# Moving a tenth of the exponentials of a two-attention kernel from ScalarE to VectorE

## The chip, the cores and the metric

One core of one Trainium2 chip. The metric is device time in microseconds (us). The kernel before takes 1167.58 us (median of four runs, 1166.66 to 1175.48). Each experiment ran in the same rounds as the kernel before, on one chip, and its ratio compares the fast runs of these rounds. The batches of experiments ran on four chips, on which the median of the kernel before was 1166.6 to 1171.4 us; times set beside each other across batches carry that difference. With one core, "slow" means only that a run lies over 1.5% above the fastest of its kernel.

## The reference

Two attention blocks over 2048 positions with a model width of 512 and 32 heads of 16. Block A is full attention; block B is causal with a window of 256. Cut to what matters:

```python
qkv = (x @ wqkv).reshape(B, S, 3, H, Dh).transpose(2, 0, 3, 1, 4)
q, k, v = qkv[0], qkv[1], qkv[2]
scores = jnp.einsum("bhqd,bhkd->bhqk", q, k) * (Dh ** -0.5)
# block B only: scores = jnp.where(mask, scores, -1e9), mask: 0 <= i - j < 256
p = softmax(scores, axis=-1)
o = jnp.einsum("bhqk,bhkd->bhqd", p, v)
out = o.transpose(0, 2, 1, 3).reshape(B, S, D) @ wo
# the outputs of A and B are joined along the last axis
```

A head is only 16 wide, so that the 32 x 2048 x 2048 exponentials of block A, not the matmuls, are the large number.

## The kernel before

Work is cut into jobs: one head, one tile of 128 keys, 512 queries. Three jobs make a *slot*: three banks of scores, one exponential over 128x1536, three weight tiles. Two slots of scores lie in PSUM (six banks), one bank holds the output accumulator `op`, and one bank, `ms`, serves everything else: projections, guards, output projections. That work is doled out in *steps* between the slots.

```python
def scores(self, slot):
    sps = self.ps.tile([P, SLOT, 512], FP32, name="sps", tag="sps", bufs=2)
    for b, jb in enumerate(slot["jobs"]):
        r = slice(32 * jb.j, 32 * jb.j + KR)          # one of four 32-row groups
        ...
        if b == 0 and self.filled < 2:                # warm-up: whole array, overwritten
            self.nc.tensor.matmul(sps[:, 0, 0:WARM], lhsT=kT[:, gg, k0:k0 + P],
                                  rhs=qT[:, gg, 0:WARM], start=True, stop=True)
        for kt, q0, q1, o in jb.subs:
            self.nc.tensor.matmul(sps[:, b, o:o + q1 - q0], lhsT=kT[r, gg, k0:k0 + P],
                                  rhs=qT[r, gg, q0:q1], start=True, stop=True,
                                  tile_position=(32 * jb.j, 0))

def exps(self, slot):
    ...
    nc.scalar.activation(out=pT[:, b:e, :n], in_=sps[:, b:e, :n], func=ACT.Exp, scale=SCALE)
    ...                                               # block B: masks, on VectorE and GpSimd

def run(self):
    ...
    for s, sl in enumerate(slots):
        self.exps(sl)
        if s + 2 < len(slots):
            self.scores(slots[s + 2])
        self.values(...)                              # weights x values, into op
        ...                                           # what is due; then steps through bank ms:
        while credit >= 1.0 and self.fill(s, tasks, done):
            credit -= 1.0
            self.filled += 1
```

A projection step is two matmuls over the whole 128x128 array; two steps fill the bank, and VectorE evacuates it. VectorE and TensorE take their instructions in the order in which the kernel issues them, as the timeline below shows: the evacuation of `op`, whose last values had ended at 383.55 us, starts at 385.90 us, after two passes issued ahead of it, and the next values start at 386.63 us, after the evacuation has ended at 386.58 us.

## Time and profile before

| | before |
|---|---|
| time | 1167.58 us |
| ScalarE busy | 1098.6 us, 94% |
| ScalarE idle before its exponentials | 32.8 us |
| VectorE busy | 298.2 us, 25% |
| mean granted TensorE clock | 0.939 |

Two more parts turned out to matter. First, from the page of the kernel before, the busy tenths of TensorE in 40 slices of the span, and the granted TensorE clock in tenths of full speed:

```profile
PE   6788888878878887777778787787777887788893
...
PEclk9999899998999898999999999999999999976777
```

TensorE is busy 79% of the time, so it has a fifth in reserve, and its clock is near full nearly everywhere (0.939 on average). Second, the largest TensorE groups of the kernel before (out<-in, shapes, count | busy us, mean ns of one | idle before, and what ended it):

```profile
L457 PE MATMUL sps<-qTa,kTa 128*128 128x512 bf16 x659 | 261.0, 396 | 159.2 <-ACT pT L480 152.9
L462 PE MATMUL sps<-qTa,kTa 32*128 32x512 bf16 x2048 | 286.5, 404 | 1.5 <-ACT pT L480 1.5
```

The first are the warm-up matmuls, whose result is thrown away; they take nearly as long as all score matmuls of block A together, because three score matmuls mostly run beside each other in different 32-row groups of the array (2048 of them at 404 ns are 827 us, in 286.5 us of busy time; three or more overlap in the records for 264 us of it). TensorE's idle time ends with ScalarE: it waits for ScalarE, not the other way.

### The profile page before, as it was taken

What the parts mean: (1) busy time and instruction counts of PE and PEld (TensorE: products, weight loads), DVE (VectorE), ACT (ScalarE), POOL (GpSimd) and SP (SyncE); (2) the same over time, 40 slices, a digit from 0 to 9 for tenths busy, and PEclk for the clock granted to TensorE, in tenths of its full rate; (3) what the DMA queues carried; (4) which work ended last, traced back from release to release, by engine and by line L of the source; (5) the groups of instructions that cost most, each with busy time, mean ns of one, the idle gap of its engine ahead of it and who ended that gap; (6) DMA issues with size and microseconds to landing.
All of it is one profiled execution on the core that took longest, in us unless ns stands there. A gap on an engine that the chain in (4) does not pass through costs nothing.

```text
span 1169.9 us, 17451 instructions
## 1 busy us (share of the span) xinstructions
PE 926.1 (79%) x6844; PEld 270.6 (23%) x6944; DVE 298.2 (25%) x674; ACT 1098.6 (94%) x841; POOL 119.0 (10%) x316
## 2 busy tenths in 40 slices
PE   6788888878878887777778787787777887788893
PEld 3222222222222222222222222222222222222221
DVE  3442121132123222222322232224223132320101
ACT  3789999998999999999999999999999999999992
POOL 4000000010001001011200121102112011210100
PEclk9999899998999898999999999999999999976777
DMA  6022421221222112211220221124012112210101
GB/s 207 10 77 75 99 83 41 61 63 52 65 78 76 45 42 65 70 47 61 83 66 32 75 76 54 39 68 118 26 48 65 65 65 69 66 43 18 57 19 55
DMA packets 72810, 73.87 MB, mean 63 GB/s; under 512 B 22688, under 2 KB 55832, under 8 KB 72728
## 3 DMA queue, kind: packets, MB, share of 16 engines
q1 hardware_dynamic: 69656, 68.83, 19.3%
q10 hardware_dynamic: 2432, 1.84, 0.5%
q0 software_dynamic: 640, 2.10, 0.5%
q8 instruction: 54, 0.88, 0.3%
q14 instruction: 28, 0.23, 0.1%
HBM read 39.06 MB, written 31.58 MB: 60 GB/s over the span
## 4 chain that ended last, share of the span: by engine, by line
ACT 62%; PE 21%; issue 11%; DVE 3%; DMA 1%; POOL 0%; ACTq 0%; another core or an unknown queue 0%; SPq 0%; DVEq 0%; POOLq 0%
ACT pT L480 61%; PE sps L462 6%; PE sps L457 6%; PE ms L202 4%; PE op L514 4%; DVE va L285 1%; DVE osb L533 1%; PE ms L591 0%; DMA den<-od 0%; DVE pT L491 0%; DMA rb<-rd 0%; PE sps L358 0%; ACT xT L610 0%; DVE padmax L394 0%; DVE kTa L392 0%
## 5 line engine op out<-in xcount | busy, mean ns | idle before, releaser
L480 ACT ACTIVATE pT<-sps 128x1536 bf16<-128x1536 f32 (+4 forms) x827 | 1088.4, 1566 | 32.8 <-PE sps L462 31.1
L457 PE MATMUL sps<-qTa,kTa 128*128 128x512 bf16 x659 | 261.0, 396 | 159.2 <-ACT pT L480 152.9
L462 PE MATMUL sps<-qTa,kTa 32*128 32x512 bf16 x2048 | 286.5, 404 | 1.5 <-ACT pT L480 1.5
L514 PE MATMUL op<-pT,va 128*32 128x512 bf16 x2048 | 216.4, 412 | 0.5 <-DVE osb L533 0.3
L493 POOL TENSOR_SCALAR_AFFINE_SELECT pT<-pT 128x256 bf16<-128x256 bf16 (+2 forms) x224 | 102.5, 475 | 967.7 <-issue 556.6
L462 PEld LDWEIGHTS <-kTa 32*128 32x128 bf16 x2048 | 68.2, 91 | 395.3 <-issue 395.3
L491 DVE TENSOR_TENSOR pT<-pT,mlo 128x256 bf16<-128x256 bf16 (+2 forms) x256 | 74.9, 334 | 136.3 <-ACT pT L480 134.9
L457 PEld LDWEIGHTS <-kTa 128*128 128x128 bf16 x659 | 64.3, 98 | 144.4 <-issue 124.4
L514 PEld LDWEIGHTS <-va 128*32 128x32 bf16 x2048 | 53.7, 94 | 125.5 <-issue 125.0
L457 PE MATMUL sps<-qTb,kTb 128*128 128x512 bf16 x128 | 51.2, 400 | 34.8 <-ACT pT L480 32.7
L533 DVE COPY osb<-op 128x512 f32<-128x512 f32 x64 | 44.2, 691 | 85.2 <-PE op L514 84.9
L462 PE MATMUL sps<-qTb,kTb 32*128 32x384 bf16 (+2 forms) x704 | 58.4, 289 | 0.0
L220 DVE CAST kst<-ms 128x512 bf16<-128x512 f32 x28 | 19.4, 691 | 141.4 <-PE ms L202 141.4
L343 DVE CAST ob<-ms 128x512 bf16<-128x512 f32 x28 | 19.4, 691 | 131.8 <-PE ms L202 131.8
L301 DVE CAST qs<-ms 128x512 bf16<-128x512 f32 x31 | 21.4, 690 | 115.1 <-PE ms L202 115.1
L514 PE MATMUL op<-pT,vb 128*32 128x384 bf16 (+2 forms) x704 | 36.6, 290 | 0.9 <-DVE osb L533 0.7
L202 PE MATMUL ms<-xT,wq 128*128 128x512 bf16 x91 | 32.2, 408 | 4.7 <-issue 4.3
L462 PEld LDWEIGHTS <-kTb 32*128 32x128 bf16 x704 | 16.9, 93 | 79.7 <-issue 79.7
L202 PE MATMUL ms<-wv,xT 128*128 128x512 bf16 x103 | 32.0, 398 | 4.2 <-issue 1.6
L202 PE MATMUL ms<-xT,wk 128*128 128x512 bf16 x89 | 30.9, 413 | 3.5 <-issue 2.7
L285 DVE CAST vb<-ms 128x512 bf16<-128x512 f32 x16 | 11.1, 692 | 84.5 <-PE ms L202 84.5
L312 DVE CAST gs<-ms 8x512 bf16<-8x512 f32 x31 | 21.0, 677 | 20.0 <-PE ms L310 20.0
(80 smaller groups left out, 274.8 us busy)
## 6 DMA issues: line engine op xcount, KB each, us to landing
od<-osb SPq DMA_DIRECT2D x64, 256.0 KB
oc<-od SPq DMA_DIRECT2D x32, 256.0 KB
rb<-rd SPq DMA_DIRECT2D x32, 256.0 KB
kTb<-kd SPq DMA_DIRECT2D x16, 256.0 KB
qTb<-qd SPq DMA_DIRECT2D x16, 256.0 KB
qd<-qs SPq DMA_DIRECT2D x31, 128.0 KB
qTa<-qd SPq DMA_DIRECT2D x15, 256.0 KB
out_dram<-ob SPq DMA_DIRECT2D x30, 128.0 KB
```

The costliest lines, as they stand in the source:

```text
L202: self.nc.tensor.matmul(bank, lhsT=lhs(c), rhs=rhs(c), start=(c == 0), stop=(c == NC - 1))
L220: copy(out=kst[:], in_=bank)
L285: copy(out=v3[:, :, 1:VP], in_=bank.rearrange("p (h d) -> p h d", d=DH))
L301: copy(out=qs[:], in_=bank)
L312: self.nc.vector.tensor_copy(out=gs[:], in_=b[0:8, :])
L457: self.nc.tensor.matmul(sps[:, 0, 0:WARM], lhsT=kT[:, gg, k0:k0 + P], rhs=qT[:, gg, 0:WARM], start=True, stop=True)
L462: self.nc.tensor.matmul(sps[:, b, o:o + q1 - q0], lhsT=kT[r, gg, k0:k0 + P], rhs=qT[r, gg, q0:q1], start=True, stop=True, tile_position=(3 ...
L480: nc.scalar.activation(out=pT[:, b:e, :n], in_=sps[:, b:e, :n], func=ACT.Exp, scale=SCALE)
L491: nc.vector.tensor_mul(out=v, in0=v, in1=self.mlo[:, 0:e - b, :])
L493: nc.gpsimd.affine_select(v, v, pattern=[[0, e - b], [-1, P]], compare_op=ALU.is_ge, fill=0.0, base=-1, channel_multiplier=1)
L514: self.nc.tensor.matmul(op[32 * jb.j:32 * jb.j + 32, q0:q1], lhsT=self.v[jb.inst, kt][:, h * VP:h * VP + 32], rhs=slot["pT"][:, b, o:o + q ...
L533: nc.vector.tensor_copy(out=osb[:], in_=self.op[i, p, g][:])
```

## The change

The intent: VectorE is 75% idle and ScalarE is the bound, so VectorE computes some exponentials. The queries are scaled so that a score, plus an offset carried in a spare row, is the number whose integer part is the bit pattern of a bf16 number: 2^x is then, but for a correction of the fraction, a conversion to a 16-bit integer. The low half-word of the fp32 number holds that fraction, and a cubic in it makes the correction. ScalarE has to produce numbers of the same scale; so it now needs a bias of -127 ln 2, which is read from a tile.

```diff
-SCALE = DH ** -0.5
+STEP = 128 * 1.4426950408889634 * DH ** -0.5
+TOP = 231 * 128.0
+LN2 = 0.6931471805599453
+POLY = (0.07826797, 3.89144693)
+FIRST_D = 4
+PACE_D = (2, 2, 2, 1)          # groups of four jobs per unit of block A, from the fifth unit on
...
-    copy(out=qs[:], in_=bank)
+    copy(out=qs[:], in0=bank, scalar1=STEP, scalar2=None, op0=ALU.mult)
...
+        self.shift = self.consts.tile([P, 1], FP32, name="shift")
+        nc.vector.memset(self.shift[:], -127 * LN2)
...
             nc.scalar.activation(out=pT[:, b:e, :n], in_=sps[:, b:e, :n], func=ACT.Exp,
-                                 scale=SCALE)
+                                 scale=LN2 / 128, bias=self.shift[:])
...
+        def step(jb):               # one step of the spare-bank work, in place of a projection step
+            ...
+            b = self.bank()
+            nc.tensor.matmul(b[:], lhsT=kT[r, g % 2, k0:k0 + P],
+                             rhs=self.qT[0, p, g // 2][r, g % 2, :], start=True, stop=True,
+                             tile_position=(32 * jb.j, 0))
+            nc.vector.tensor_copy(out=y[:, half, :], in_=b[:])
+            ...                     # after every second job, three passes over 128x1024:
+            def first():    # h = (low - 65536) * low
+                nc.vector.scalar_tensor_tensor(out=st["h"][:], in0=low, scalar=-65536.0,
+                                               in1=low, op0=ALU.add, op1=ALU.mult)
+            def second():   # h = (low + 65536 c) * h
+                ...
+            def third():    # pattern = h * c' + y, converted to uint16
+                ...
+            self.dq += [first, second, third]
...
+            for _ in range(min(2, len(self.dq))):    # per slot, after the steps
+                self.dq.pop(0)()
...
-                if kind == "d":
-                    nc.vector.tensor_mul(out=v, in0=v, in1=self.mlo[:, 0:e - b, :])
-                else:
-                    nc.gpsimd.affine_select(...)
+                nc.gpsimd.affine_select(...)         # all masks of block B on GpSimd
-QRING = (3, 4)
-KRING_B = 10
-VRING_B = 12
+QRING = (3, 3)
+KRING_B = 8
+VRING_B = 10
... (other rings one buffer shorter, to make room)
```

## The prediction

> **What bounds the kernel now.** I read the page first: the busy shares, then the slices, the chain of waits and the costly groups; then the idle reasons and single ScalarE instructions in time order. The busy shares and the chain that ended last:
>
> ```profile
> PE 926.1 (79%) x6844; PEld 270.6 (23%) x6944; DVE 298.2 (25%) x674; ACT 1098.6 (94%) x841; POOL 119.0 (10%) x316
> ...
> ACT  3789999998999999999999999999999999999992
> ...
> ACT 62%; PE 21%; issue 11%; DVE 3%; DMA 1%; POOL 0%; ACTq 0%; another core or an unknown queue 0%; SPq 0%; DVEq 0%; POOLq 0%
> ```
>
> ScalarE is busy 94% of the span and full in every slice but the first few and the last; VectorE has 75% of the span free. The groups by shape tell what ScalarE does (busy is a union in time, so overlap of neighbours is counted once):
>
> ```profile
> L480 ACT ACTIVATE pT<-sps 128x1536 bf16<-128x1536 f32 x782 | 1058.6, 1608 | 30.4 <-PE sps L462 28.9 <-DVE pT L491 1.0
> L559 DVE TENSOR_TENSOR oTa<-oc,rb 128x512 bf16<-128x512 f32 x16 | 10.9, 681 | 30.1 <-DMA rb<-rd 30.1
> L533 DVE COPY osb<-op 128x512 f32<-128x512 f32 x64 | 44.2, 691 | 85.2 <-PE op L514 84.9
> L493 POOL TENSOR_SCALAR_AFFINE_SELECT pT<-pT 128x256 bf16<-128x256 bf16 x84 | 38.2, 468 | 455.2 <-ACT pT L480 271.6 <-issue 178.2 <-POOL pT L493 4.6
> ```
>
> One exponential of three score banks (a slot) shows 1.608 us, but 782 of them fill only 1058.6 us: their real pitch is 1058.6/782 = 1.354 us. ScalarE waits just 30.4 us in all, mostly on the scores. The span is therefore 26.7 us until the first exponential, about 1089 us of exponentials with about 32 us of gaps, and some 22 us after the last. The bound is the number of ScalarE exponentials times their pitch.
>
> [...] the old exponential has an immediate bias, the new one reads the bias from a tile. The trace of the kernel before has both kinds, in its start-up, on 512 elements:
>
> ```profile
> 12.85 0.69 ACT L389 ACTIVATE kTa<-op,ones 128x512 bf16<-128x512 f32 x1 [1.41 <-PE op L202]
> 13.44 1.00 ACT L610 COPY xT<-sps 128x1024 bf16<-128x1024 bf16 x1
> ...
> 26.20 0.58 ACT L285 CAST va<-op 128x512 bf16<-128x512 f32 x1 [1.86 <-PE op L202]
> 26.68 5.49 ACT L480 ACTIVATE pT<-sps 128x1536 bf16<-128x1536 f32 x4
> ```
>
> The columns are start, duration and work. With a bias tile (ones): 0.69 us, and the next instruction starts 0.59 us later. Without: 0.58 us, and the next starts 0.48 us later. So about 0.10 us is added, not only to the duration but to the time until the next may start[...]. [...]
>
> **The change, part by part.**
> Removed: from the fifth unit of the full attention on, groups of four jobs leave ScalarE in the pattern 2, 2, 2, 1: 28 units x 7/4 = 49 groups = 196 of 2048 jobs. The order of instructions confirms it: 811 slots become 746, 827 exponentials 762. At 1.354 us a slot that is 65.3 x 1.354 = 88 us less ScalarE work, all of it on the bounding engine.
>
> Added on ScalarE: the bias tile, 762 x about 0.10 us = 76 us, if the 0.10 us stays in the pitch of instructions that follow each other closely. ScalarE's exponentials then go 1089 - 88 + 76 = 1077 us: nearly nothing is gained. This term decides the case.
>
> Added on VectorE: 196 evacuations of 128x512 fp32 from PSUM at 0.691 us = 135 us; 98 x 3 = 294 scalar_tensor_tensor of 1024 elements at 1067 + 148 = 1.215 us = 357 us (estimated from the 512-element row). Taken away: 256 mask multiplications (86 x 0.381 + 84 x 0.339 + 86 x 0.282 us), which overlap to the 74.9 us of their group. Sum 298 - 75 + 135 + 357 = 715 us, some 62% of the span: beside ScalarE's work, not above it. Those masks go to GpSimd, 256 x about 0.475 us = 122 us, so POOL some 240 us; the window jobs are now consumed three slots after their exponential instead of two, which should hide that.
>
> Moved on TensorE: the 196 score matmuls stay, in the single spare PSUM bank instead of the slots; 70 warm-up matmuls of 0.396 us (787 become 717) vanish with their slots, 28 us, off the path.
>
> Stalls: VectorE takes work in order. In the new order a polynomial job comes about every 1.7 slots while a group is served. Two jobs cost 2 x 0.691 + 3 x 1.215 = 5.0 us plus the old work, (298-75)/811 = 0.275 us a slot, 0.9 us: 5.9 us in 3.4 slots, which last 4.6 us at the old pitch and 4.9 us at the new one. VectorE falls about 1 us behind per pair. The spare bank is then freed late, TensorE, also in order, stands before it, and the next scores come late; only two score buffers cover this. Over a whole unit (about 23 slots) VectorE has time to catch up, so I take 1 us per unit lost, some 28 us, chosen within 10 to 60.
>
> Sum with the bias term: 1168 - 88 + 76 + about 10 to 25 (part of the old 32 us of gaps is absorbed by the longer pitch) = 1165 to 1180. Sum without it: 1168 - 88 + 10 to 60 = 1090 to 1140.
>
> **The rivals.**
> (a) The bias read hides. Back-to-back exponentials start some 0.25 us before the one ahead has ended (1.608 against 1.354), so the read of 128 scalars might happen under the stream of its predecessor. Against: both measured pairs start after idle and the follower still comes 0.10 us later. The time would be near 1115 us, with VectorE stalls the main loss. I give it 35%.
> (b) The bias costs its full 0.10 us each time: 1165 to 1180 us; ScalarE's share stays over 93%, with 65 fewer slots. 65%.
> (c) VectorE becomes the bound. [...] I give this 15%, across both (a) and (b).
> (d) The masks on GpSimd become a wait for the values. A window unit has 15 masks, about 7 us, in four slots, about 5.5 us, with three slots of grace[...]. A few us at most, in (a) and (b) alike.
>
> **Range and chances.** Weighing 1115 (about 30%), 1172 (about 55%) and over 1180 (about 15%) gives a middle near 1160. The threshold for faster is 1144 us, for slower 1191. Rival (a) nearly always lies below the first; (b) mostly between the two, with a tail above if VectorE's stalls reach 30 us. Time 1158 us, 8 in 10 between 1100 and 1198.
>
> **What would show each step.** Pitch of the 128x1536 exponential (group busy over count): 1.45 means the bias is paid, 1.35 that it hides. [...] Busy: VectorE near 715, POOL near 240, ScalarE near 1085 (a: 1010). The idle time before exponentials: if it rises from 30 us to over 60, and TensorE's waits name the evacuation of the spare bank, the stall term was too small. Wrong altogether would be: a bias that costs more or less than 0.10 us, or VectorE delaying the accumulator's evacuation so that values, then scores, stand still for several slots each unit.

## The result, and the profile after

The changed kernel takes 1283.45 us (median of four runs, 1281.05 to 1286.34) against 1167.58 us. Ratios here and below are the mean time of one kernel's fast runs over that of the other's of the same rounds, so not quite the ratio of the medians: 1.0977, with a 95% interval of 1.0924 to 1.103. It is 116 us slower, and outside the predicted range.

The page of the changed kernel: busy times, busy tenths and clock by slice, and the chain that ended last by engine.

```profile
PE 1089.9 (85%) x6890; PEld 275.9 (22%) x6890; DVE 717.1 (56%) x910; ACT 1099.8 (86%) x776; POOL 241.9 (19%) x575
...
DVE  4431357736775574754675557466554764557551
ACT  4899988898988989989888898987898879888893
...
PEclk9999887687777978879678787975787769855567
...
PE 36%; ACT 31%; DVE 16%; issue 12%; POOL 3%; DMA 2%; ACTq 0%; POOLq 0%; DVEq 0%
```

ScalarE's busy time is the same as before (1099.8 against 1098.6 us) although it has 65 exponentials fewer, but it is now only 86% of the span: the bound has moved. The chain of waits, which was ScalarE 62% and TensorE 21%, is now TensorE 36%, ScalarE 31%, VectorE 16%. And the granted clock of TensorE has fallen from 0.939 to 0.784, from the fifth slice on, about where the polynomials begin.

The groups of the changed kernel:

```profile
L495 ACT ACTIVATE pT<-sps,shift 128x1536 bf16<-128x1536 f32 (+2 forms) x762 | 1089.6, 1526 | 140.5 <-PE sps L475 85.2
...
L536 DVE COPY dy<-ms 128x512 f32<-128x512 f32 x196 | 134.6, 687 | 136.3 <-PE ms L533 135.5
...
L546 DVE SCALAR_TENSOR_TENSOR dh<-dy 128x1024 f32<-128x1024 uint16 x98 | 123.2, 1257 | 3.3
L533 PE MATMUL ms<-qTa,kTa 32*128 32x512 bf16 x196 | 98.4, 502 | 31.3 <-DVE dy L536 29.3
```

VectorE's new work costs what the prediction said. What differs is the idle time ahead of the exponentials: 140.5 us where it was 32.8. That is 108 of the 116 us. How such a gap arises, in the changed kernel in order of time (start, duration, work, idle time before and its releaser):

```profile
383.23 1.30 DVE L546 SCALAR_TENSOR_TENSOR dh<-dy 128x1024 f32<-128x1024 uint16 x1
...
384.02 0.61 PE L475 MATMUL sps<-qTa,kTa 32*128 32x512 bf16 x3
384.56 1.42 DVE L550 SCALAR_TENSOR_TENSOR dh<-dy,dh 128x1024 f32<-128x1024 uint16 x1
385.90 0.68 DVE L601 COPY osb<-op 128x512 f32<-128x512 f32 x1
...
386.63 0.63 PE L582 MATMUL op<-pT,vb 128*32 128x384 bf16 x8 [2.01 <-DVE osb L601]
...
387.34 1.54 ACT L495 ACTIVATE pT<-sps,shift 128x1536 bf16<-128x1536 f32 x1 [2.16 <-PE op L582]
```

The evacuation of the accumulator stands behind two polynomial passes on VectorE. The next values start at 386.63 us, when it is done (386.58 us), and TensorE stands 2.01 us before them. ScalarE stands 2.16 us. The scores that its next exponential reads had ended at 384.63 us (first PE line); what ends its wait is the values. They free a buffer of weights (`pT`, of which there are six), so that a free buffer is most likely what it lacked; no run changed their number. The next scores stand behind the same values. Over the whole trace, who waited for whom (us in total, times, longest):

```profile
ACT pT L495 <- PE sps L475: 85.2, 121, 3.0
...
ACT pT L495 <- PE op L582: 45.9, 49, 2.8
...
PE ms L533 <- DVE dy L536: 29.3, 25, 3.4
...
PE op L582 <- DVE osb L601: 20.1, 18, 2.2
```

After the first 30 us, all waits of TensorE that VectorE ended come to 74.5 us here and to 20.0 us in the kernel before. The rise is half of the 108 us that ScalarE lost, so these waits alone do not account for the gaps. And the same place by stretches of 5 us (busy us of each engine with its instruction count, then the granted clock):

```profile
375.00:380.00 5.00, 4.21 (x35) 1.33 (x32) 4.71 (x6) 5.00 (x8) 5.00 (x10) 0.90 0.91 207
380.00:385.00 5.00, 4.61 (x21) 0.85 (x20) 4.93 (x6) 3.76 (x5) 5.00 (x7) 0.50 0.20 56
...
395.00:400.00 5.00, 5.00 (x26) 0.93 (x25) 3.39 (x4) 3.73 (x3) 0.00 (x0) 0.50 0.40 126
...
405.00:410.00 5.00, 4.26 (x32) 1.23 (x30) 1.02 (x3) 5.00 (x4) 0.00 (x0) 1.00 0.10 30
```

From 380 to beyond 400 us the clock is at one half. In the third row TensorE is busy for all of 5.00 us and gets 26 matmuls done; in the last, 32 in 4.26 us. ScalarE (fourth pair) is busy 3.73 us of 5 in the first case and 5.00 in the second. In the third row, at half clock, TensorE is the slower of the two. Over the whole trace a score matmul of block A takes 602 ns at half clock and 385 ns at full (medians). In this trace and in that of the kernel before the clock takes just two values, 0.5 and 1.0, in 66 and 42 stretches that are multiples of 3.41 us, but for the last, which the end cuts off; so the mean tells the time at half clock: 2 x (1 - 0.784) x 1279.2 = 553 us, against 2 x (1 - 0.939) x 1169.9 = 143 us before. Adding up gaps and clock records of the changed trace, 124 of the 140 us of idle time before exponentials lie in the half-clock stretches.

The third row is busy for 5.00 of 5.00 us and still at half clock, so that busy time alone does not tell what the clock does. What else might becomes a question below.

### The profile page after: what moved, and what is told of

Its sections match the earlier page's. It is cut to its first block, busy times and chain, and to the rows that moved or that the text cites. A ratio compares the mean times of both kernels' runs of the same rounds, so it can differ in the third digit from the quotient of the medians.

```text
span 1279.2 us, 17755 instructions
## 1 busy us (share of the span) xinstructions
PE 1089.9 (85%) x6890; PEld 275.9 (22%) x6890; DVE 717.1 (56%) x910; ACT 1099.8 (86%) x776; POOL 241.9 (19%) x575
## 4 chain that ended last, share of the span: by engine, by line
PE 36%; ACT 31%; DVE 16%; issue 12%; POOL 3%; DMA 2%; ACTq 0%; POOLq 0%; DVEq 0%
ACT pT L495 31%; PE sps L475 9%; PE sps L470 9%; PE op L582 9%; PE ms L214 5%; DVE dh L546 4%; PE ms L533 4%; DVE dy L536 3%; DVE dh L550 3%; POOL pT L506 2%; DVE pD L556 2%; DVE osb L601 1%; DVE va L297 1%; DMA qd<-oc 1%; DMA rb<-rd 1%
## 5 line engine op out<-in xcount | busy, mean ns | idle before, releaser
L495 ACT ACTIVATE pT<-sps,shift 128x1536 bf16<-128x1536 f32 (+2 forms) x762 | 1089.6, 1526 | 140.5 <-PE sps L475 85.2
L506 POOL TENSOR_SCALAR_AFFINE_SELECT pT<-pT 128x256 bf16<-128x256 bf16 (+2 forms) x480 | 224.0, 507 | 946.8 <-ACT pT L495 946.6
L470 PE MATMUL sps<-qTa,kTa 128*128 128x512 bf16 x593 | 281.8, 475 | 70.8 <-ACT pT L495 66.9
L475 PE MATMUL sps<-qTa,kTa 32*128 32x512 bf16 x1852 | 303.8, 473 | 1.3 <-ACT pT L495 1.2
L536 DVE COPY dy<-ms 128x512 f32<-128x512 f32 x196 | 134.6, 687 | 136.3 <-PE ms L533 135.5
L546 DVE SCALAR_TENSOR_TENSOR dh<-dy 128x1024 f32<-128x1024 uint16 x98 | 123.2, 1257 | 3.3
L533 PE MATMUL ms<-qTa,kTa 32*128 32x512 bf16 x196 | 98.4, 502 | 31.3 <-DVE dy L536 29.3
L550 DVE SCALAR_TENSOR_TENSOR dh<-dy,dh 128x1024 f32<-128x1024 uint16 x98 | 121.7, 1241 | 3.4
L556 DVE SCALAR_TENSOR_TENSOR pD<-dh,dy 128x1024 uint16<-128x1024 f32 x98 | 120.5, 1230 | 1.8
L313 DVE TENSOR_SCALAR qs<-ms 128x512 bf16<-128x512 f32 x31 | 21.4, 691 | 84.0 <-PE ms L214 84.0
```

The lines of the kernel that those rows point to most:

```text
L506: nc.gpsimd.affine_select(v, v, pattern=[[0, e - b], [s, P]], compare_op=ALU.is_ge, fill=0.0, base=base, channel_multiplier=-s)
L533: nc.tensor.matmul(b[:], lhsT=kT[r, g % 2, k0:k0 + P], rhs=self.qT[0, p, g // 2][r, g % 2, :], start=True, stop=True, tile_position=(32 * ...
L536: nc.vector.tensor_copy(out=y[:, half, :], in_=b[:])
L546: nc.vector.scalar_tensor_tensor(out=st["h"][:], in0=low, scalar=-65536.0, in1=low, op0=ALU.add, op1=ALU.mult)
L550: nc.vector.scalar_tensor_tensor(out=st["h"][:], in0=low, scalar=65536.0 * POLY[1], in1=st["h"][:], op0=ALU.add, op1=ALU.mult)
L556: nc.vector.scalar_tensor_tensor(out=out.bitcast(U16), in0=st["h"][:], scalar=POLY[0] * 2.0 ** -41, in1=flat, op0=ALU.mult, op1=ALU.add)
```

## The experiments

Three causes offered themselves. **Bias**: the exponential with a bias tile has a longer pitch. **V**: VectorE, in order, holds TensorE up, either through the order of its queue or through the amount of its work. **H**: the clock is lost because a step of the spare bank that used to bring two whole-array projection matmuls now brings one 32-row score matmul; in g1 and h4, the same for narrower warm-up matmuls. In the expectations, **R** stands for a limit beside these: TensorE has too little time in reserve to catch up or to take more matmuls. The first expectations speak of A (the tile costs pitch, and VectorE's stalls lower the clock), B (the longer pitch itself lowers the clock) and C (scaling, masks or rings do). In the table, "cubic" is three passes per pair of jobs; clock and idle time (before exponentials) are those of the profiled run.

| run | bias | jobs moved | passes | other | median us of fast runs | ratio to before (95%) | clock | idle us |
|---|---|---|---|---|---|---|---|---|
| changed kernel | tile | 196 | 3 | | 1283.45 | 1.098 (1.092 to 1.103) | 0.784 | 140.5 |
| e1_imm | number | 196 | 3 | | 1242.37 | 1.062 (1.055 to 1.070) | 0.800 | 168.3 |
| e2_nopoly | tile | 0 | | | 1257.35 | 1.074 (1.066 to 1.082) | 0.879 | 48.3 |
| e3_nopoly_imm | number | 0 | | | 1167.88 | 0.997 (0.991 to 1.004) | 0.934 | 30.4 |
| e4_light | tile | 196 | 1 | | 1208.70 | 1.034 (1.026 to 1.043) | 0.803 | 91.8 |
| e5_imm_heat1 | number | 196 | 3 | 1 whole-array matmul per job | 1286.24 | 1.098 (1.089 to 1.108) | 0.812 | 210.8 |
| e6_imm_heat2 | number | 196 | 3 | 2 of them | 1294.80 | 1.111 (1.100 to 1.121) | 0.862 | 220.4 |
| e7_imm_light | number | 196 | 1 | | 1136.95 | 0.972 (0.960 to 0.984) | 0.852 | 92.8 |
| e8_imm_light_heat2 | number | 196 | 1 | 2 of them | 1147.04 | 0.982 (0.975 to 0.990) | 0.951 | 88.3 |
| g1_imm_warm256 | number | 196 | 3 | narrower warm-ups | 1231.73 | 1.054 (1.049 to 1.059) | 0.733 | 156.1 |
| g2_imm_pop1 | number | 196 | 3 | one pass per slot | 1207.17 | 1.031 (1.025 to 1.038) | 0.802 | 134.6 |
| g3_imm_half_pop1 | number | 112 | 3 | one pass per slot | 1176.23 | 1.005 (0.997 to 1.013) | 0.879 | 75.0 |
| g4_imm_half_pop1_heat1 | number | 112 | 3 | the same, 1 of them | 1168.86 | 1.002 (0.995 to 1.010) | 0.895 | 87.6 |
| h1_imm_direct | number | 196 | 0 | | 1122.87 | 0.959 (0.953 to 0.966) | 0.903 | 55.5 |
| h2_imm_direct_heat1 | number | 196 | 0 | 1 of them | 1100.87 | 0.942 (0.935 to 0.948) | 0.972 | 37.2 |
| h3_imm_two_pop1 | number | 196 | 2 | one pass per slot | 1174.67 | 1.005 (1.001 to 1.009) | 0.840 | 106.7 |
| h4_nopoly_imm_warm128 | number | 0 | | narrow warm-ups | 1230.20 | 1.052 (1.049 to 1.056) | 0.634 | 75.2 |
| i1_centred_heat1 | number | 196 | 0 | centred, 1 of them | 1102.17 | 0.943 (0.936 to 0.950) | none | |
| i2_centred_heat1_three | number | 336 | 0 | centred, 1 of them | 1127.04 | 0.971 (0.965 to 0.978) | 0.871 | 109.9 |

All gave outputs that passed the comparison with the reference, also those with fewer passes, which are less exact. Six kernels had slow runs; over all four runs the medians of e4, e7, g4, h1, i1 and i2 are 1213.07, 1148.28, 1173.97, 1125.92, 1114.70 and 1132.13 us, and the later expectations quote 1148 for e7. The profiles of e4, e7 and g4 fell in slow runs. In their fast runs the clock was 0.817 to 0.840, 0.875 and 0.892, and 0.909 to 0.922, so their clock and idle time in the table lean to the slow side.

### Bias tile or number, with and without polynomials

```diff
 # e1_imm, e3_nopoly_imm
-                                 scale=LN2 / 128, bias=self.shift[:])
+                                 scale=LN2 / 128, bias=-127 * LN2)
 # e2_nopoly, e3_nopoly_imm
-PACE_D = (2, 2, 2, 1)
+PACE_D = (0,)
```

e1_imm: 

> The changed kernel with the exponential's bias as an immediate number instead of a tile; nothing else. Theory A (the bias tile costs 0.09 us of pitch per exponential, and TensorE's clock falls because VectorE holds TensorE up): the pitch of the 128x1536 exponential goes from 1.43 back to 1.34 us, ScalarE's busy time to about 1020 us, but the clock stays near 0.78 and the idle time before exponentials grows, so 1230 to 1275 us. Theory B[...]: the clock returns to above 0.90 and the time falls to 1090 to 1140 us.

e2_nopoly: 

> The changed kernel with no group moved to VectorE (the pattern set to 0); the bias tile, the masks on GpSimd and the smaller rings stay. Theory A: 811 exponentials at a pitch of 1.43 us and few stalls: 1168 + 827 x 0.09 = 1240 us less what hides in old gaps, so 1225 to 1245 us, clock above 0.90. Theory B: the clock falls to about 0.8 here too, idle before exponentials over 80 us, 1270 us or more.

e3_nopoly_imm: 

> The changed kernel with no group moved and the bias immediate: what is left is the scaled scores, masks on GpSimd, smaller rings. Both theories: the time of the kernel before, 1160 to 1180 us, clock near 0.94. A third one (C: the large scaled numbers or the masks and rings lower the clock or stall): 1190 us or more, with a clock below 0.90 or waits on GpSimd.

Without polynomials the tile costs 1257 against 1168 us, 89 us, more than A said and less than B. The group of the large exponential by shape, first of e3_nopoly_imm, then of e2_nopoly:

```profile
L495 ACT ACTIVATE pT<-sps 128x1536 bf16<-128x1536 f32 x782 | 1060.5, 1567 | 29.9 <-PE sps L475 20.2 <-PE op L582 9.3
```

```profile
L495 ACT ACTIVATE pT<-sps,shift 128x1536 bf16<-128x1536 f32 x782 | 1133.3, 1608 | 47.6 <-PE sps L475 28.2 <-PE op L582 15.8
```

Busy over count is 1060.5/782 = 1.356 us with the number and 1133.3/782 = 1.449 us with the tile: 0.093 us for each, back to back, nothing hidden. Read the busy union, not the mean: the means, 1.567 and 1.608, differ by less than half of it. The other 18 us are idle time, with the clock down to 0.879.

e3 is as fast as the kernel before (ratio 0.997): scaled scores, all masks on GpSimd and shorter rings cost nothing that these runs show. So theory C falls, and all 116 us belong to the bias tile and to the polynomials. The two do not add up: the tile costs 89 us without polynomials but 41 us with them (1283 against 1242 us), where part of it replaces idle time (168.3 us in e1, 140.5 us with the tile). e1 against e3, at the same bias, is the polynomials alone: 1242 against 1168 us, 74 us lost where 88 were to be won. ScalarE's exponentials fell from 1090.2 to 1022.5 us, but its idle time rose from 30.4 to 168.3. Theory B, that the bias lowers the clock, falls as the main cause, since the clock stays at 0.800 in e1; the tile does cost some clock by itself (0.879 to 0.905 in the runs of e2, 0.934 to 0.956 in those of e3).

### Fewer passes on VectorE

```diff
 # e4_light, e7_imm_light, e8_imm_light_heat2: one pass, output = max(y, y)
-            self.dq += [first, second, third]
+            self.dq += [only]
 # h3_imm_two_pop1: quadratic correction
+QUAD = 0.3437
...
-            self.dq += [first, second, third]
+            self.dq += [first, third]
-                                               scalar=POLY[0] * 2.0 ** -41, in1=flat,
+                                               scalar=QUAD * 2.0 ** -25, in1=flat,
 # h1_imm_direct: the evacuation writes the 16-bit result, no pass
-            nc.vector.tensor_copy(out=y[:, half, :], in_=b[:])
+            nc.vector.tensor_copy(out=pD[:, jb.j, :].bitcast(U16), in_=b[:])
```

e4_light: 

> The changed kernel with one VectorE pass per pair of polynomial jobs instead of three (less exact on purpose): VectorE loses 196 instructions of 1.25 us, 245 us of busy time. Theory A: TensorE no longer waits on VectorE, the clock comes back above 0.88, idle before exponentials falls from 140 to below 60 us, 1165 to 1200 us. Theory B: the bias tile is still there, the clock stays near 0.8 and the time above 1240 us.

e7_imm_light: 

> Immediate bias and one VectorE pass instead of three (less exact on purpose), no extra matmuls. Theory H: the clock stays near 0.8 and the scores late: 1150 to 1200 us, idle before exponentials over 100 us. Theory V: with VectorE out of the way the saving of 88 us shows, 1085 to 1120 us, clock above 0.9.

h1_imm_direct: 

> Immediate bias; the evacuation of each polynomial score bank writes the 16-bit result itself, without any pass (the fraction is not corrected, less exact on purpose): VectorE has 0.69 us per job instead of 2.55. Theory V-amount: against 1148 us with one pass another 98 x 1.28 = 125 us of VectorE go, stalls nearly end, 1095 to 1125 us. Theory R/H (the single score matmul and the clock remain): 1130 to 1150 us.

With the immediate bias the time goes 1242 (three passes), 1137 (one; two fast runs only), 1123 us (none). Those 119 us are what the passes cost; hardly any of it is ScalarE's work, whose exponentials keep busy for 1009 to 1023 us in all three. So VectorE's time per job is the largest single cause. It isn't the only one: V alone would have had 1085 to 1120 us at one pass. The clock comes back in part when VectorE is relieved: in the fast runs from 0.794 to 0.800 in e1 to 0.875 and 0.892 in e7 and 0.883 to 0.903 in h1, against 0.939 in the kernel before. So VectorE's stalls are one part of the clock's fall, and the 119 us include what that part costs. H alone, which had e7 near 0.8 and at 1150 us or more, missed as well; e4 lies outside both of its forecasts.

### Order or amount

```diff
 # g2_imm_pop1, g3, g4, h3
-            for _ in range(min(2, len(self.dq))):
+            for _ in range(min(1, len(self.dq))):
 # g3_imm_half_pop1, g4_imm_half_pop1_heat1
-PACE_D = (2, 2, 2, 1)
+PACE_D = (1,)
```

g2_imm_pop1: 

> Immediate bias, three passes, at most one pass issued per slot instead of two, so that the evacuation of the spare bank stands behind at most one pass. Theory V-order (it is the order in VectorE's queue that holds TensorE up): 1150 to 1200 us, idle before exponentials below 100 us. Theory V-amount (VectorE's total in a burst of polynomial jobs, 5.1 us per pair, is above what the slots last, in any order): 1220 to 1250 us, little changed.

h3_imm_two_pop1: 

> Immediate bias, one pass issued per slot, and a quadratic correction in two passes instead of the cubic in three (about 0.25 per cent off at most, near the step of the 16-bit result). V-amount: between three passes (1207 us) and one (1148 us): 1165 to 1190 us. If only the order mattered, two passes at one per slot would stay near 1200 us.

g3_imm_half_pop1: 

> Immediate bias, one group per unit instead of 7/4 (112 jobs instead of 196, 774 slots) and one pass per slot. 37 slots fewer at 1.354 us are 50 us less than the 1168 us without polynomials. Theory V-amount: bursts of four jobs are over before VectorE is far behind, stalls fall to a third or less, 1135 to 1165 us. If each polynomial job costs the same as now ((1242 - 1168) / 196 = 0.38 us): 1168 + 112 x 0.38 = 1210 us.

One pass per slot instead of two, the same work: 1207 against 1242 us. So order accounts for 35 us, less than V-order expected and more than V-amount did, and amount for more: at that order, two passes instead of three give 1175, and none (h1) 1123. 112 jobs instead of 196 give 1176, so the cost falls faster than the jobs do (1190 would be proportional to the 39 us that g2 loses; the 1210 of the expectation takes e1's loss, at two passes per slot), but less than V-amount hoped (1135 to 1165), and there is no gain over the kernel before. The cubic can be made harmless here; I found no setting at which it pays.

### The clock: more and fewer whole-array matmuls

```diff
 # e5 (1), e6 (2), e8 (2), g4 (1), h2 (1): ahead of the score matmul, into the same bank
+            for _ in range(N):
+                nc.tensor.matmul(b[:], lhsT=kT[:, g % 2, k0:k0 + P],
+                                 rhs=self.qT[0, p, g // 2][:, g % 2, :], start=True, stop=True)
             nc.tensor.matmul(b[:], lhsT=kT[r, g % 2, k0:k0 + P],
 # g1_imm_warm256: 256; h4_nopoly_imm_warm128: 128, without polynomials
-WARM = 512
+WARM = 256
```

h4_nopoly_imm_warm128: 

> No polynomials, immediate bias, warm-up matmuls 128 columns wide instead of 512: less of the array in use, nothing on VectorE. Theory H: the clock falls below 0.75 with VectorE idle, and scores come late in the cold stretches: 1180 to 1230 us against 1168. Theory V (the clock falls because TensorE waits): clock stays above 0.9, 1155 to 1170 us.

This run has no polynomials, so that VectorE is busy 231.6 us, and only the warm-up matmuls are narrower. The busy times and the clock by slice, first of e3_nopoly_imm, then of this run:

```profile
PE 942.9 (81%) x6960; PEld 267.5 (23%) x6960; DVE 231.4 (20%) x420; ACT 1100.4 (94%) x841; POOL 195.0 (17%) x575
...
PEclk8999999899999999999999999889999999776787
```

```profile
PE 1072.3 (87%) x6960; PEld 290.2 (24%) x6960; DVE 231.6 (19%) x420; ACT 1114.0 (91%) x841; POOL 196.3 (16%) x575
...
PEclk8995777855555755556575865555565875555566
```

The clock falls to 0.634 and the time rises by 62 us over e3, though TensorE was given *less* to do. So the clock alone can cost 62 us, nearly as much as the polynomials (74 us), and it falls without more waiting for VectorE: after the first 30 us, VectorE ended 21.5 us of TensorE's waits here and 19.2 us in e3. TensorE is busy for 87% of this span and at half clock for 73% of it (2 x (1 - 0.634)), so idle time does not account for the half clock here; what the matmuls fill of the array is the other candidate.

The trace of the changed kernel says the same in stretches of 3.41 us, the grid of the clock's records. Between its first and last polynomial score matmul, of the half-clock stretches in which at least one of these starts, 93 of 93 are followed by another at half clock; of those without, 30 of 59. Half-clock stretches that lead back to full clock hold on average 1.6 matmuls of projections or guards, those that don't hold 0.1. In this trace the clock comes back beside projection steps, and never right after a stretch in which a polynomial step starts.

A count over the kept traces goes further. Weight the columns of each matmul by its share of 128x128 (its form in the record: 128*128 for a projection matmul, which counts 512, and 32*128 for a score matmul, which counts 128), split it by time where it crosses a border, and add up by stretch. In the changed kernel the half-clock stretches that lead to full clock have 2982 to 3528, those that don't have at most 3031. Over all 19 traces that record the clock, one line at 3050 sorts 1940 of 2023 half-clock stretches rightly (161 of 162 in the changed kernel, 30 of 42 in the kernel before); calling all of them "stays at half" gets 1606, and no line through TensorE's busy share gets more than that. The line was fitted afterwards, and more than half of its misses lie in h4 (21), the kernel before (12) and g1 (11). A stall and a lost whole-array matmul both lower this sum, so that V and H are not rivals in it. It is a fit to these traces; no run tested it.

e5_imm_heat1: 

> The changed kernel with the immediate bias and, in front of each of the 196 polynomial score matmuls, one matmul over the whole array (128x128 by 512, result overwritten). Theory H ([...] a polynomial step uses a fill slot for one 32-row matmul where a projection step brings two whole-array ones): cold time falls from 499 us to below 300, clock above 0.86, time 1120 to 1190 against 1242 us without. Theory V (TensorE stands behind VectorE, the clock is a result of that): 196 more matmuls of 0.3 to 0.5 us on a TensorE that is already late, 1250 to 1290 us, clock 0.8.

e6_imm_heat2: 

> The same with two whole-array matmuls in front of each polynomial score matmul, as many as a projection step has. Theory H: cold time below 200 us, clock above 0.90, time 1100 to 1170. Theory V: 1260 to 1330 us.

e8_imm_light_heat2: 

> Immediate bias, one VectorE pass, and two whole-array matmuls per polynomial job. Theory H: both obstacles gone, clock above 0.92, 1090 to 1125 us, the best of all so far. Theory V: as the run without the extra matmuls or up to 50 us slower.

h2_imm_direct_heat1: 

> The same with one whole-array matmul ahead of each polynomial score matmul. If the clock is what remains (H): clock above 0.93 and 10 to 30 us faster than without. If TensorE's reserve remains (R): same time within 10 us though the clock rises.

g4_imm_half_pop1_heat1: 

> The same and one whole-array matmul ahead of each polynomial score matmul. If with less VectorE work the clock is what is left: clock above 0.93, 10 to 25 us faster than without it. If TensorE's reserve is what is left: the same time or up to 20 us slower.

g1_imm_warm256: 

> Immediate bias, three passes, and each warm-up matmul (whole array, result overwritten) 256 columns wide instead of 512, which takes some 0.1 us off TensorE's work per slot. Theory R (TensorE has so little reserve per slot that it can't make up for its waits on VectorE): 1190 to 1225 us against 1242. Theory H[...]: the clock falls below 0.75 and the time rises to 1260 to 1330 us.

Whole-array matmuls ahead of the polynomial ones (196 of 392 ns each in h2) raise the clock in each case: 0.800, 0.812, 0.862 for none, one, two with three passes; from 0.875 and 0.892 to 0.951 or more in fast runs with one pass; 0.903 to 0.972 with none. So H is right about the direction of the clock, though e5 and e6 stay below the 0.86 and 0.90 that it asked for. But the time follows only where VectorE is out of the way: with three passes it *rises* by 44 and 52 us, with one pass it shows no gain (1131 and 1143 us in the fast runs of e7, 1146 to 1156 in e8), with none it falls by 22 us. With half the jobs (g4 against g3) it is the same, as R said. H's times for e5, e6 and e8 were wrong, and V's were right. And g1, with a lower clock still (0.733, as H expected), was not slower than e1: the ratios are 1.054 and 1.062, with intervals that overlap, where R had hoped for 17 to 52 us and H for a loss (score matmuls of 256 and 512 columns take 285 and 404 ns in the kernel before, the 0.1 us that R counted on). That TensorE, already late behind VectorE, has no room for more matmuls is how I read these runs; no run isolates it.

Of the best run, h2_imm_direct_heat1, the busy times, the clock and the chain:

```profile
PE 969.2 (89%) x7086; PEld 288.2 (26%) x7086; DVE 363.5 (33%) x616; ACT 1017.9 (93%) x776; POOL 202.4 (19%) x575
...
PEclk8999899999999999999999998799999999999996
...
ACT 53%; PE 26%; issue 13%; DVE 5%; DMA 2%; POOL 1%; ACTq 0%; DVEq 0%; POOLq 0%
```

ScalarE is the bound again, at 93% of a shorter span, with 37.2 us idle. It takes 1100.87 us, 5.8% less than the kernel before: about 68 of the 88 us that 65 slots are worth.

### A version to use, and how far it goes

```diff
 # i1_centred_heat1: as h2, and
-            nc.vector.tensor_copy(out=pD[:, jb.j, :].bitcast(U16), in_=b[:])
+            nc.vector.tensor_scalar(out=pD[:, jb.j, :].bitcast(U16), in0=b[:], scalar1=-5.5,
+                                    scalar2=None, op0=ALU.add)
 # i2_centred_heat1_three: also
-PACE_D = (2, 2, 2, 1)
+PACE_D = (3,)
+            self.filled += 1         # in the polynomial step: no warm-up in the next slot
-                st["pD"] = self.tile([P, GH, 512], BF16, "pD", 3)
+                st["pD"] = self.tile([P, GH, 512], BF16, "pD", 6)
```

i1_centred_heat1: 

> As the best run so far (immediate bias, evacuation straight to the 16-bit result, one whole-array matmul ahead of each polynomial score matmul), but the evacuation also subtracts 5.5 steps, so that the uncorrected fraction is at most about 3 per cent off either way instead of 6 per cent high. One instruction as before: 1095 to 1108 us. If an addition in the evacuation costs more than a copy (it did 0.06 us where it read a tile): up to 10 us slower.

i2_centred_heat1_three: 

> The same with three groups per unit from the fifth on (336 jobs, 700 slots), six result buffers, and no warm-up matmul in the slot after a polynomial job, since the whole-array matmul ahead of it stands in for it. If ScalarE stays the bound: another 47 slots at 1.354 us, 63 us less, 1035 to 1055 us. If TensorE becomes the bound (two more matmuls of 0.3 us per job): 1070 to 1110 us, idle before exponentials above 80 us.

i1's two fast runs took 1095.59 and 1108.76 us, and a third, 1120.65 us, counts as slow; the ratio, 0.943, is that of h2 (0.942), so centring shows no cost (the evacuation takes 692 ns with the addition in i1's trace and 691 ns in h2's; the one that adds from a tile takes 751 ns in the kernel before). The uncorrected fraction is up to 6% high, centred about 3% off either way, on a tenth of block A's weights; whoever needs bf16-exact weights can't use it. One of its runs, the profiled one, took 2485.73 us with matmuls of nearly twice their usual length (the score matmul 891 ns against 473 in the changed kernel). Its trace holds no clock record at all, so the 1.0 that the record gives it is not a measured clock; one run of the kernel before took 1678.68 us in another round. I left both out as slow and have no explanation.

i2 moved 336 jobs and is slower than i1, at 1127 us (ratio 0.971 against 0.943), outside both of its forecasts. Its chain by engine, and its exponentials:

```profile
PE 48%; ACT 24%; DVE 16%; issue 8%; DMA 2%; POOL 0%; another core or an unknown queue 0%; ACTq 0%; DVEq 0%
...
L495 ACT ACTIVATE pT<-sps 128x1536 bf16<-128x1536 f32 (+3 forms) x715 | 961.5, 1454 | 109.9 <-PE sps L475 78.6
```

ScalarE has only 961.5 us of exponentials left, but 109.9 us idle ahead of them, and TensorE is twice ScalarE's share of the chain. Here it is mostly TensorE, with a single score matmul and a whole-array one for each job, that sets the end. The clock is low again (0.871), and only 225 of the changed kernel's 593 warm-up matmuls of block A are left; no run tells whether that is why.

A first form of i2 with three result buffers deadlocked when it was built and was not run, by my account. Still open: what sets the clock, since the line at 3050, fitted to these traces, misses 83 of 2023 stretches; whether the three-pass version would gain from a second spare bank (not tried) or from more buffers of weights; and why one pass gains nothing from the better clock (e7, e8).

## Why the prediction was wrong

- **The bias term was right for one exponential, and too high for the whole.** It said 0.10 us for each, 76 us together, and that rival (a), a hidden read, was the less likely. Measured: 0.093 us for each. That e2 against e3 gives 76.5 us of busy time (1166.7 against 1090.2 us) is luck, since they have 827 exponentials and not 762. In the changed kernel the tile added 67.1 us of busy time (1089.6 against 1022.5 us in e1) and 41 us of time.
- **VectorE's and GpSimd's sums were right.** 715 us predicted, 717.1 measured; about 240 and 241.9. The passes took 1.23 to 1.26 us where 1.215 was estimated. That estimate splits the 681 ns of the 512-element row into 148 ns that stay and 533 ns that double; reductions over 2 and 4 elements take 146 and 148 ns in the trace of the kernel before. Rival (c), VectorE as the bound, did not occur: it was busy 56% of the span.
- **The masks on GpSimd**, rival (d): e3 shows no loss. They took 409 ns on average there and 507 ns in the changed kernel; no run tests why.
- **The saving of 88 us was too high as busy time.** From e3 to e1 ScalarE's exponentials lost 67.7 us. An exponential that follows a gap occupies 1.45 us by itself, and in a train the next one starts after 1.33 us (medians in e1 and e3); 241 of e1's large exponentials follow a gap of over 0.1 us, and 75 of e3's, so that overlap of neighbours is lost.
- **The step that failed is "Stalls".** It put the loss at 1 us per unit, "some 28 us, chosen within 10 to 60", and counted just 10 to 25 of it beside the bias. The idle time before exponentials rose by 108 us in the changed kernel and by 138 us in e1 against e3. The prediction's own ratio, 5.9 us of VectorE work in 4.9 us, was sound: in the changed kernel a group's third polynomial matmul starts 5.99 us after its first (mean of 49 groups; 4.91 us in h1, which has no passes), so the kernel went at about VectorE's pace, 1.1 us late per pair. The error was to let VectorE catch up and to count that once per unit. Counted for each of the 98 pairs it is 108 us; that this meets the measured rise so closely is partly luck, as the clock has a share in it.
- **What was missing altogether is TensorE's clock.** "Moved on TensorE" counted 28 us of vanished warm-up matmuls as off the path and did not ask what the warm-up was for. The changed kernel was at half clock for 553 instead of 143 us, in stretches of 17 us on average, and in the stretch shown TensorE was slower than ScalarE at half clock, so that little could be made up. h4 shows that the clock alone can cost 62 us; how much of the changed kernel's 108 us it cost is not separated from the stalls that lowered it.
- **The checks named in the prediction worked.** It said that idle time over 60 us, with TensorE waiting for the spare bank's evacuations, would show the stall term too small; these waits are 29.3 us in the list above. It also named as "wrong altogether" that VectorE delays the accumulator's evacuation, so that values and then scores stand still. The timeline shows just that (20.1 us of TensorE's waits), but the prediction gave it no time.

## What to carry to other kernels

Before moving work to an idle engine, ask which engine will stand behind that work and how much reserve it has; a VectorE at 56% was enough to hold up a kernel whose TensorE was at 79%. In this kernel TensorE's clock was part of the budget: narrower warm-up matmuls alone took it from 0.934 to 0.634 and cost 62 us (e3, h4), and one whole-array matmul per polynomial job raised it from 0.903 to 0.972 (h1, h2). So where a kernel carries warm-up matmuls, count what a change takes away of whole-array work. And where ScalarE is the bound, try numbers in place of tiles for the constants of back-to-back exponentials: the tile cost 0.093 us each here (1.449 against 1.356).
